# Bias rows computed four softmax units sooner in a fused attention and FFN kernel

## The chip, the cores and the metric

The kernel runs on one core of one Trainium2 chip. The metric is the device time of one execution in microseconds (us); several runs are timed and the median is given. One further execution is profiled.

## The reference, cut to what matters

Attention with a relative-position bias, then layer norm and a two-layer FFN with a residual. Batch 4, 8 heads, 576 positions, head size 64, model width 512, FFN width 2048, all float32.

```python
scores = scale * np.matmul(q, k.transpose(0, 1, 3, 2))
rel = pos[:, None] - pos[None, :]
x = (np.log1p(np.abs(rel)) / np.log1p(np.maximum(pos[:, None], 1.0)))[..., None]
bias = np.maximum(x @ w1 + b1, 0.0) @ w2          # (576, 576, 8), the same for every batch
scores = scores + bias.transpose(2, 0, 1)[None]
attn = softmax(scores)
x = (attn @ v) as (4, 576, 512)
xn = (x - mean) / np.sqrt(var + 1e-06) * g_ln
out = x + np.maximum(xn @ w_ch1, 0.0) @ w_ch2
```

The bias doesn't depend on the batch. It is computed once, kept in DRAM and read back for each batch.

## The kernel before

**Units.** The 576 query rows are cut into five chunks: 0 to 3 of 128 rows, and 4 of 64 rows. A *unit* is one batch, one chunk and one head (for chunk 4 two heads), 144 in all, numbered by `u` in the order of `ORD` (L213): chunk 4 of batches 0 and 1 (units 0 to 7), chunk 0 of all batches (8 to 39), chunk 4 of batches 3 and 2 (40 to 47), chunk 1 (48 to 79), chunk 2 (80 to 111), chunk 3 (112 to 143). The main loop (L861) writes one unit after the other; `cfirst[c]` is a chunk's first unit.

**A unit.** `qk` (L377) multiplies queries and keys on TensorE into the PSUM tile `sps`. `softmax1` (L422) subtracts the bias on VectorE into a float32 tile `t` and takes the row's minimum at once (L434), takes the exponential on ScalarE (L438) and a float16 high half (L443). `softmax2` (L446) makes the low half on VectorE (L462, L464) and transposes both by a DMA on SP's queue (L470, into `pt`, or into `wend` for every fifth unit from 35 on). `pv` (L496) multiplies with V on TensorE (L480). V's float16 halves are made by `v_max` and `split_v` (L362), eleven to four units and four units before to two units after a batch first needs them; for batch 1 that is unit 64, for batch 0 unit 72.

**The FFN.** It runs beside attention, as its tiles come ready: `ffn_w1` (L709) into `hps`, an eviction on ScalarE (L714) and a low half on VectorE (L717) into the hidden tile `hh`, then `ffn_w2` (L736) into `y`, which VectorE adds up (L747). `mbank` says how many such steps a unit gets. After unit 143 only FFN is left.

**Bias rows.** A *group* is 16 query rows of the bias for all heads, 36 in all, in the order of `gorder`: chunk 4's four (32 to 35), then 0 to 31. `bias_relu` makes four tiles `r` of the hidden layer, here one on VectorE (L162) and three on ScalarE (L160). `bias_mm`, one unit later, multiplies them with the output weights on TensorE (L181), evicts them in two parts on ScalarE into `ev` (L187), and writes `ev` to DRAM (`nb`, L211) on SP's queue. The tiles `t`, `r`, `ev` and layer norm's `u` share one pool of seven buffers. Each `r` holds 128 x (SEQ or fewer) elements, so a group's cost hangs a little on its number.

**When a group is begun.** Seven are done before the loop and five more in units 0 to 4. In later units at most one is begun, when fewer than `bneed` have been (L920 to L927). `gend[c]` is the count of groups at the end of chunk c.

**Loads.** `issue_loads` (L277) issues keys, queries and V on the queue of GpSimd, and the bias back from DRAM (`ldb`, L326) on SP's queue, seven units before the unit that needs it and only when all groups of its chunk have been through `bias_mm`. SP's queue thus carries, in order: row writes, bias loads, the transposes, and the output.

**Order.** The program's order is a starting point: a planner settles each engine's order from simulated times, and adds the waits.

Of the kernel before, what the change touches and what calls it, by code (L numbers as in the profile page):

```python
# [22 lines left out]
def kernel(  # L23
# [114 lines left out]
    def after(ins, dep):  # L138
        if dep is not None:
            tc.add_manual_dep(ins.ins, dep.ins.name,  # L140
                              mybir.DependencyInfo(mybir.DependencyClass.Sync,
                                                   mybir.DependencyReason.DATA),
                              reason="pace")
# [73 lines left out]
    for n, (b, c) in enumerate(ORD):  # L217
# [6 lines left out]
    cfirst = {c: min(u for (_, cc), u in ustart.items() if cc == c) for c in range(5)}  # L224
    gorder = [g for c in corder for g in range(8 * c, min(36, 8 * c + 8))]
    gend = {c: sum(len(range(8 * x, min(36, 8 * x + 8))) for x in corder[:corder.index(c) + 1])
            for c in range(5)}
# [178 lines left out]
    def spin(n, last=None):  # L406
        ps = ps_h.tile([128, 512], F32, tag="h", name="spin")
        ones = one_sb.bitcast(BF16)
        for _ in range(n):
            m = T.matmul(out=ps[:, 0:256], lhsT=ones[:, 0:128], rhs=ones, start=True, stop=True)  # L410
            if last is None:
                tc.keep_in_program_order(m)
            else:
                tc.add_manual_dep(m.ins, last.ins.name,
                                  mybir.DependencyInfo(mybir.DependencyClass.NoSync,
                                                       mybir.DependencyReason.DATA),
                                  reason="order")
            last = m
# [3 lines left out]
    def softmax1(u):  # L422
        if not 0 <= u < NU:
            return
        b, c, h = units[u]
        ps = st.pop(u)
        t = ep.tile([128, EW], F32, tag="e", name="t")[:, 0:SEQ]
        m = small.tile([128, 1], F32, tag="m", name="m")
        key = (seg[vis[u]], c, h)
        bias = bt[key]  # L430
        buse[key] -= 1
        if not buse[key]:
            bfree[0] += 1
        ttri[u] = V.tensor_tensor_reduce(out=halves(t), in0=ps[:, :, 0:HS], in1=halves(bias), scale=-0.125,  # L434
                               scalar=3e38, op0=ALU.add, op1=ALU.min, accum_out=m)
        if h == 0:
            l8[b, c] = small.tile([128, NH], F32, tag="l8", name="l8")
        S.activation(t, t, AF.Exp, bias=m, scale=-1.0, accum_out=l8[b, c][:, h:h + 1])  # L438
        if nat_pv(b, c):
            et[u] = (t, None)  # L440
            return
        e16 = e16p.tile([128, 1152], F16, tag="e16", name="e16")
        S.activation(e16[:, 0:SEQ], t, AF.Copy, scale=E_SCALE)  # L443
        et[u] = (t, e16)

    def softmax2(u):  # L446
        if not 0 <= u < NU:
            return
        t, e16 = et.pop(u)
        if e16 is None:  # L450
            p = ptp.tile([128, 10, 128], F16, tag="pt", name="pt")
            p = p.rearrange("p a b -> p (a b)").bitcast(F32)
            pm = ps_y.tile([128, 512], F32, tag="y0", name="ptm")
            pl = ps_h.tile([128, 512], F32, tag="h", name="ptl")
            for j in range(4):
                T.transpose(pm[:, 128 * j:128 * j + 128], t[:, 128 * j:128 * j + 128], id_sb)
            T.transpose(pl[0:64, 0:128], t[:, 512:576], id_sb)
            S.activation(p[:, 0:512], pm, AF.Copy)
            S.activation(p[0:64, 512:640], pl[0:64, 0:128], AF.Copy)
            pt[u] = p  # L460
            return
        V.scalar_tensor_tensor(out=e16[:, 640:1152], in0=t[:, 0:512], scalar=E_SCALE,  # L462
                               in1=e16[:, 0:512], op0=ALU.mult, op1=ALU.subtract)
        V.scalar_tensor_tensor(out=e16[:, 576:640], in0=t[:, 512:576], scalar=E_SCALE,  # L464
                               in1=e16[:, 512:576], op0=ALU.mult, op1=ALU.subtract)
        if u >= 35 and u % 5 == 0:
            p = wslot[NF].bitcast(F16)[:, 0:1152].rearrange("p (a b) -> p a b", b=128)
        else:
            p = ptp.tile([128, 10, 128], F16, tag="pt", name="pt")[:, 0:9]
        SY.dma_start_transpose(out=p, in_=e16)  # L470
        pt[u] = p
# [270 lines left out]
    def ffn_y():  # L742
        while yq:
            k, g, t, y, last = yq.pop(0)
            b, c = tiles[blocks[k][t]]
            x = xt[b, c].rearrange("p a d -> p (a d)")
            V.scalar_tensor_tensor(out=x, in0=y, scalar=ycs[:, g:g + 1], in1=x,  # L747
                                   op0=ALU.mult, op1=ALU.add)
            if last:
                if c < 4:  # L750
                    SY.dma_start(out=out[b, c * 128:c * 128 + 128, :], in_=x)
                else:
                    SY.dma_start(out=out[b:b + 2, 512:576, :], in_=x)
# [24 lines left out]
    def flush_lo():  # L778
        if state["lo"]:
            state["lo"]()  # L780
            state["lo"] = None
# [46 lines left out]
    def flush():  # L828
        later[0], later[1] = later[1], []
        for fn in later[0]:  # L830
            fn()
# [28 lines left out]
    u = 0  # L860
    while u < NU + 6 or jobs or cur_job or pend or yq:  # L861
        if u >= NEARLY:
            ffn_y()
        if u in FILL:
            with tc.high_priority(offset=-600):
                spin(FILL[u], lastpv[0])
        softmax1(u)
        if u == 0:
            for ins in gate:
                after(ins, ttri[0])  # L870
            gate.clear()
            gate_on[0] = False
        ustep[0] = u
        issue_loads(u)
        softmax2(u - 1)
        flush()
        for _ in range(2):
            if wload:
                load_w()
        for _ in range(8):  # L880
            if wdec and 32 - len(wdec) < 2 + (4 * max(0, u - 1) + 2) // 3:
                f, i = wdec.pop(0)
                decode_w(f, i)
                if i == 1 and f + 1 == GROUPS[GOF[f]][1]:
                    w_scale(GOF[f])
        while mm_done[0] < ngroup:
            bias_mm(gorder[mm_done[0]])
            mm_done[0] += 1
        if u % 2:
            first = qk(u + 1)  # L890
            if u >= 27 and first is not None:
                after(first, ttri[max(ttri)])
            qk(u + 2)
        while npv <= u - (LAG if u < 38 else LAG + 1):
            if pv(npv):
                lnq.append([u, len(avail_at) + len(lnq)])
            npv += 1
        for fn in todo.pop(u, []):
            fn()
        for qq in range(4):  # L900
            if wdone[0] >= 8 * qq + 8 and qq not in wready_at:
                wready_at[qq] = u
        if u < NU + 9:
            nav = len([a for a in avail_at if a <= u])
            goal = sum(2 * NF * len(bl) // 4 for bl in blocks if bl[-1] < nav)
            nxt = min((steps_av[bl[-1]] for bl in blocks if bl[-1] >= nav), default=NU + 9)
            mbank += max(0.0, (goal - (ntot - nmicro) - mbank)) / max(1, nxt - u)
            mbank = min(mbank, 2.0)
        else:
            mbank = 1.0  # L910
        flush_lo()
        ffn_y()
        while mbank >= 1.0:
            if not ffn_micro(u):
                break
            mbank -= 1.0
            nmicro -= 1
            if mbank >= 1.0:
                ffn_y()
        bneed = NP + 1 + u if u < 8 else 12  # L920
        for c in (1, 2, 3):
            bneed = max(bneed, gend[c] - 8 + min(8, (u - cfirst[c] + 34) * 8 // 24))
        if u < 28:
            bneed = min(bneed, 12)
        if ngroup < min(36, bneed):
            bias_relu(gorder[ngroup], 1 if u >= 24 else 2)
            ngroup += 1  # L927
        for _ in range(2):
            if wspl:
                split_w(*wspl.pop(0))  # L930
        for it in list(lnq):
            if it[0] == u - 1:
                ln1(it[1])
            if it[0] == u - 2:
                ln2(it[1])
                avail_at.append(u + (3 if u < NEARLY else 2))
                lnq.remove(it)
        u += 1
# [53 lines left out]
```

## Time and profile before

| | |
|---|---|
| timed runs | 686.31, 686.28, 683.54 us; median 686.28 |
| profiled execution | 679.99 us, of which the span from first to last instruction is 678.2 us |
| granted TensorE clock, mean | 0.985 of full speed |
| busy: TensorE matmul, VectorE, ScalarE | 647.7, 457.8, 392.0 us |

PE is TensorE's matmuls, PEld its weight loads, DVE VectorE, ACT ScalarE, POOL GpSimd, SP the SyncE queue that issues DMAs. A busy share tells how long an engine had an instruction running; it does not tell in which stretch it was the one that the others waited for.

### The profile page before, as it was taken

Reading aid. Unit: us, or ns where it says so; the run is one execution under the profiler, and the core shown is the slowest. Engines: PE = TensorE matmul, PEld = TensorE weight load, DVE = VectorE, ACT = ScalarE, POOL = GpSimd, SP = SyncE. Lnnn points to the kernel's source line nnn. Section 1 sums busy time; section 2 is a strip of 40 time slices with the busy share of each in tenths; the row PEclk is TensorE's granted clock in tenths of the full one; section 3 lists DMA queues with packets and bytes.
Section 4 is the critical chain, followed back from the end, with each engine's and each line's share of the span. In section 5 each row is a group of like instructions: output and inputs, shape, how many; then the busy total and the mean of one; then the engine's idle time right before and its main releaser. Section 6 shows DMA issues by size and latency. Waiting matters only on the chain.

```text
span 678.2 us, 19142 instructions
## 1 busy us (share of the span) xinstructions
PE 647.7 (96%) x7929; PEld 448.4 (66%) x7929; DVE 457.8 (68%) x1061; ACT 392.0 (58%) x777; POOL 97.4 (14%) x163
## 2 busy tenths in 40 slices
PE   6889996998999889999899999999999999999997
PEld 4447774676466666666667766666776677677775
DVE  6588999778757567686766575757576676766322
ACT  5565847478957447787764577576554455444110
POOL 5312321011000011111101110111011120000000
PEclk9989997899999999999899999999999999999999
DMA  8999885444659996868869789789996976744100
GB/s 312 294 404 331 307 294 161 143 91 115 143 122 148 223 246 156 173 156 164 172 149 239 134 183 181 136 197 181 201 200 144 166 153 125 121 98 87 33 16 17
DMA packets 186955, 117.24 MB, mean 173 GB/s; under 512 B 163956, under 2 KB 164084, under 8 KB 186868
## 3 DMA queue, kind: packets, MB, share of 16 engines
q1 hardware_dynamic: 177124, 81.00, 55.8%
q0 software_dynamic: 9600, 34.84, 16.6%
q8 instruction: 62, 1.02, 0.6%
q10 hardware_dynamic: 144, 0.18, 0.1%
q14 instruction: 25, 0.20, 0.1%
HBM read 60.51 MB, written 15.63 MB: 112 GB/s over the span
## 4 chain that ended last, share of the span: by engine, by line
PE 50%; DVE 0%; ACT 0%; issue 0%
PE hps L709 19%; PE y L736 18%; PE sps L391 6%; PE xps L480 6%; PE bps L181 1%; DVE v L369 0%; DVE x L747 0%; DVE e L462 0%; ACT e L443 0%; DVE x L516 0%; ACT t L438 0%; DVE e L464 0%
## 5 line engine op out<-in xcount | busy, mean ns | idle before, releaser
L709 PE MATMUL hps<-xT,w 128*128 128x128 f16 x3240 | 196.4, 220 | 5.8 <-DVE hh L717 2.6
L709 PEld LDWEIGHTS <-w 128*128 128x128 f16 x3240 | 184.6, 98 | 11.5 <-issue 5.2
L736 PE MATMUL y<-w,hh 128*128 128x512 f16 x810 | 189.1, 381 | 1.9 <-ACT hh L714 1.8
L438 ACT ACTIVATE t<-t,m 128x576 f32<-128x576 f32 x144 | 111.0, 771 | 132.8 <-DVE m L434 132.2
L736 PEld LDWEIGHTS <-hh 128*128 128x128 f16 x864 | 79.7, 98 | 90.6 <-ACT hh L714 3.3
L462 DVE SCALAR_TENSOR_TENSOR e<-t,e 128x512 f16<-128x512 f32 x120 | 82.8, 690 | 81.8 <-ACT e L443 81.5
L434 DVE CUSTOM_DVE_ANT_0 t<-sps,ldb 128x576 f32<-128x576 f32 x144 | 105.9, 753 | 31.4 <-PE sps L391 21.2
L391 PE MATMUL sps<-kf,qf 64*128 64x288 f32 (+1 forms) x640 | 96.6, 436 | 3.5 <-DVE m L434 3.5
L443 ACT ACTIVATE e<-t 128x576 f16<-128x576 f32 x120 | 80.8, 679 | 9.8 <-DMA pt<-e 3.5
L714 ACT ACTIVATE hh<-hps 128x512 f16<-128x512 f32 x72 | 42.0, 583 | 53.4 <-PE hps L709 47.9
L717 DVE SCALAR_TENSOR_TENSOR hh<-hps,hh 128x512 f16<-128x512 f32 x72 | 49.4, 687 | 34.0 <-ACT hh L714 33.5
L391 PEld LDWEIGHTS sps<-kf,qf 64*128 64x128 f32 (+1 forms) x640 | 48.2, 176 | 35.6 <-issue 17.5
L480 PEld LDWEIGHTS <-pt 128*128 128x128 f16 (+1 forms) x1456 | 49.3, 100 | 30.5 <-issue 24.9
L747 DVE SCALAR_TENSOR_TENSOR x<-y,ycs,x 128x512 f32<-128x512 f32 x58 | 43.4, 748 | 32.2 <-PE y L736 32.0
L480 PE MATMUL xps<-v,pt 128*128 128x64 f16 (+1 forms) x1456 | 59.0, 195 | 1.9 <-DMA pt<-e 1.1
L291 POOL DMA_DIRECT2D kf<-in_k_s_dram x56 | 31.1, 556 | 161.4 <-PE sps L391 114.3
L304 POOL DMA_DIRECT2D qf<-in_q_main_dram x32 | 18.5, 577 | 162.4 <-PE xps L480 82.6
L187 ACT ACTIVATE ev<-bps,cb_sb,par_sb 128x144 f32<-128x144 f32 (+27 forms) x48 | 26.0, 593 | 26.2 <-PE bps L181 26.0
L160 ACT ACTIVATE r<-psi_sb,par_sb 128x448 f32<-128x448 f32 (+23 forms) x72 | 39.7, 614 | 0.0
L569 POOL TENSOR_SCALAR rs<-mv 128x1 f32<-128x1 f32 x18 | 9.9, 549 | 146.3 <-DVE mv L568 138.3
L438 ACT ACTIVATION_READ_ACCUMULATOR t<-t,m 128x1 f32 x144 | 27.0, 188 | 0.0
L181 PE MATMUL bps<-r,nw_sb 128*32 128x448 f32 (+24 forms) x200 | 26.9, 494 | 0.0
(121 smaller groups left out, 641.4 us busy)
## 6 DMA issues: line engine op xcount, KB each, us to landing
kf<-in_k_s_dram POOLq DMA_DIRECT2D x56, 288.0 KB, 4.8
w<-in_w_ch_dram SPq DMA_DIRECT2D x22, 512.0 KB, 8.7
ldb<-nb SPq DMA_DIRECT2D x32, 288.0 KB, 4.5
qf<-in_q_main_dram POOLq DMA_DIRECT2D x32, 256.0 KB, 4.6
nb<-ev SPq DMA_DIRECT2D x24, 296.0 KB, 3.4
vf<-in_v_p_dram POOLq DMA_DIRECT2D x16, 320.0 KB, 7.5
out_dram<-x SPq DMA_DIRECT2D x18, 256.0 KB, 2.1
wend<-in_w_ch_dram SPq DMA_DIRECT2D x8, 512.0 KB, 4.8
```

The source lines that it names most:

```text
L160: S.activation(r[:, 0:n], psi_sb[:, 0:n], AF.Relu, bias=pr_sb[:, g4:g4 + 1], scale=1.0)
L391: m = T.matmul(out=o, lhsT=l, rhs=kk, start=True, stop=True, tile_position=(64 * hf, 64 * e))
L434: ttri[u] = V.tensor_tensor_reduce(out=halves(t), in0=ps[:, :, 0:HS], in1=halves(bias), scale=-0.125, scalar=3e38, op0=ALU.add, op1=ALU.mi ...
L438: S.activation(t, t, AF.Exp, bias=m, scale=-1.0, accum_out=l8[b, c][:, h:h + 1])
L443: S.activation(e16[:, 0:SEQ], t, AF.Copy, scale=E_SCALE)
L462: V.scalar_tensor_tensor(out=e16[:, 640:1152], in0=t[:, 0:512], scalar=E_SCALE, in1=e16[:, 0:512], op0=ALU.mult, op1=ALU.subtract)
L480: T.matmul(out=o, lhsT=p[:, m], rhs=v[:, j, a, :], start=(i == 0), stop=(i == len(ops) - 1))
L709: T.matmul(out=h[:, idx * n:idx * n + n], lhsT=w[:, wo + kk * 128:wo + kk * 128 + 128], rhs=xT[k][:, xo + kk, 0:n], start=(i == 0), stop=( ...
L714: S.activation(hh[:, 0], h, AF.Relu)
L717: V.scalar_tensor_tensor(out=hh[:, 1], in0=h, scalar=0.0, in1=hh[:, 0], op0=ALU.max, op1=ALU.subtract)
L736: T.matmul(out=yps[k][t], lhsT=hh[:, a, o:o + 128], rhs=w[:, wo:wo + 512], start=(f == f0 and i == 0), stop=(f == f1 - 1 and i == 2))
L747: V.scalar_tensor_tensor(out=x, in0=y, scalar=ycs[:, g:g + 1], in1=x, op0=ALU.mult, op1=ALU.add)
```

## The change

One constant of the formula that says how many groups should have been begun by unit u: 34 becomes 38, in the line for chunks 1 to 3.

```diff
         bneed = NP + 1 + u if u < 8 else 12
         for c in (1, 2, 3):
-            bneed = max(bneed, gend[c] - 8 + min(8, (u - cfirst[c] + 34) * 8 // 24))
+            bneed = max(bneed, gend[c] - 8 + min(8, (u - cfirst[c] + 38) * 8 // 24))
         if u < 28:
             bneed = min(bneed, 12)
         if ngroup < min(36, bneed):
```

A chunk's eight groups are spread over 24 units, one in three; the constant says how many units ahead of the chunk's first unit that begins.

## Rows read from the trace of the kernel before

**Rows 1.** The page's first part: busy us, share of span, instructions.

```profile
PE 647.7 (96%) x7929; PEld 448.4 (66%) x7929; DVE 457.8 (68%) x1061; ACT 392.0 (58%) x777; POOL 97.4 (14%) x163
```

**Rows 2.** Busy time by stretch, cut at units 28, 35, 40, 48, 56...

```profile
core 0: us, PE busy (x) PEld busy (x) DVE busy (x) ACT busy (x) POOL busy (x), PEclk, DMA share, GB/s
150.40:199.20 48.80, 46.12 (x492) 26.90 (x490) 36.11 (x78) 37.93 (x73) 4.92 (x8) 1.00 0.58 126
199.20:215.90 16.70, 16.70 (x208) 11.04 (x207) 12.43 (x32) 14.27 (x30) 0.62 (x1) 1.00 0.83 111
215.90:250.70 34.80, 31.70 (x496) 22.11 (x489) 20.48 (x49) 15.13 (x30) 5.12 (x9) 1.00 1.07 226
250.70:282.00 31.30, 30.87 (x437) 21.06 (x434) 22.49 (x54) 22.39 (x48) 4.28 (x7) 1.00 0.81 185
282.00:314.30 32.30, 32.30 (x421) 22.32 (x419) 23.92 (x58) 26.09 (x52) 4.89 (x8) 1.00 0.76 165
314.30:350.20 35.90, 33.90 (x410) 23.39 (x408) 24.83 (x59) 25.49 (x52) 5.03 (x8) 0.95 0.76 154
350.20:379.40 29.20, 29.20 (x379) 20.91 (x377) 19.67 (x46) 15.11 (x31) 2.82 (x4) 1.00 0.90 209
379.40:475.50 96.10, 96.10 (x1229) 65.18 (x1227) 62.57 (x148) 64.72 (x126) 13.27 (x24) 1.00 0.86 168
505.20:534.70 29.50, 29.50 (x386) 21.13 (x386) 19.77 (x48) 14.64 (x29) 4.93 (x8) 1.00 0.78 145
```

**Rows 3.** Timeline, group 21: start us, us, engine, line, operation, tiles.

```profile
314.41 1.54 ACT L160 ACTIVATE r<-psi_sb,par_sb 128x353 f32<-128x353 f32 x3
...
320.41 0.80 PE L181 MATMUL bps<-r,nw_sb 128*32 128x353 f32 x8
...
321.35 1.09 ACT L187 ACTIVATE ev<-bps,cb_sb,par_sb 128x352 f32<-128x352 f32 x2 [0.49 <-PE bps L181]
```

**Rows 4.** TensorE's waits from 199 to 250 us: total us, times, longest.

```profile
PE hps L709 <- DVE hh L717: 1.3, 1, 1.3
PE xps L480 <- DMA wend<-e: 0.5, 1, 0.5
```

**Rows 5.** TensorE's waits from 250.7 to 617 us, complete.

```profile
PE y L736 <- ACT hh L714: 1.6, 1, 1.6
PE xps L480 <- DVE x L543: 0.4, 1, 0.4
PE xps L480 <- DVE x L516: 0.4, 1, 0.4
```

**Rows 6.** Timeline, units 66 to 68: four rows between 322 and 334 us.

```profile
322.97 0.63 SPq L211 DMA_DIRECT2D nb<-ev  x1
...
329.41 0.76 DVE L434 CUSTOM_DVE_ANT_0 t<-sps,ldb 128x576 f32<-128x576 f32 x1 [1.29 <-DMA nb<-ev]
...
332.48 0.58 ACT L714 ACTIVATE hh<-hps 128x512 f16<-128x512 f32 x1
...
333.11 0.61 PE L736 MATMUL y<-w,hh 128*128 128x512 f16 x2 [1.57 <-ACT hh L714]
```

**Rows 7.** The tile `ev`: its row writes, issue to landing.

```profile
DMA to landing us min/median/max: 3.0/3.9/10.8
```

**Rows 8.** Busy time by stretch, 4 us each, columns as in rows 2.

```profile
330.00:334.00 4.00, 2.15 (x23) 0.69 (x20) 3.88 (x9) 3.29 (x6) 0.54 (x1) 1.00 0.48 110
334.00:338.00 4.00, 3.86 (x61) 3.85 (x61) 3.96 (x9) 2.88 (x6) 0.90 (x2) 0.57 1.14 150
```

**Rows 9.** Timeline, SP's queue and TensorE around the chunk 1 bias loads.

```profile
223.53 0.58 SPq L211 DMA_DIRECT2D nb<-ev  x1
...
228.76 1.28 SPq L326 DMA_DIRECT2D ldb<-nb  x3
...
230.21 2.01 SPq L470 DMA_TRANSPOSE wend<-e  x1
...
236.10 0.63 PE L480 MATMUL xps<-v,wend 128*64 128x64 f16 x28 [0.53 <-DMA wend<-e]
```

**Rows 10.** SP queue's waits over the span: total us, times, longest.

```profile
SPq L326 <- DMA nb<-ev: 10.5, 4, 4.6
```

## The prediction

> **What bounds the kernel now.** I read the page's busy shares first: the matrix engine has a matmul in flight for 647.7 of 678.2 us and VectorE and ScalarE stay far below it [rows 1]. A mean over the whole span hides stages, so I then cut the trace at the starts of every eighth softmax unit (the 144 instructions of L434, in order; unit 40 starts at 215.9 us, unit 48 at 250.7 us, and so on) and asked for each engine's busy time in every piece [rows 2]. The reader is to see two kinds of piece. Eight units without a bias group take 29.2 us (units 72 to 79) or 29.5 us (units 112 to 119), with no idle time on TensorE at all. Call it 29.35. Where groups fall in, the piece is longer by about 1 us for each: units 56 to 63 hold three and take 32.3, so 0.98 each; units 80 to 103 hold eight and take 96.1, so (96.1 - 3 x 29.35) / 8 = 1.0 each. The eight matmul records of one group take 0.80 us [rows 3]. So from unit 48 on a group costs its own work on TensorE and nearly nothing else, and that work is the same wherever it stands.
>
> What a shift can change is therefore only the time that TensorE loses. I listed its waits for the stretch that the change touches. From 199 to 250 us it waits 1.3 us for the low half of an FFN hidden tile and 0.5 us for a transpose [rows 4]; the piece of units 40 to 47 has 34.80 - 31.70 = 3.1 us of idle time in all [rows 2], so another 1.3 us have no releaser in the list. From 250.7 to 617 us it waits 2.4 us in all [rows 5]. Beside the idle time there is the clock: the granted share is 1.00 in every piece but that of units 64 to 71, where it is 0.95 [rows 2].
>
> That piece is the odd one. It holds three groups and should take 29.35 + 3 x 0.98 = 32.3 us, but takes 35.9, so 3.6 us are lost. The timeline shows how [rows 6]. Group 21's row write is issued at 322.97; the softmax of unit 68 on VectorE is to reuse the slot of that group's `ev` and starts at 329.41, when the write has landed, 6.4 us after its issue, against a median of 3.9 us for such writes [rows 7]. ScalarE's queue is then late, the hidden tile's eviction starts at 332.48, and TensorE stands idle until 333.11. In the 4 us after that its granted clock is 0.57 of 2.4 GHz, so part of them ran at 1.2 GHz: 0.43 x 4 = 1.72 us [rows 8]. Idle time of 2.0 us in the piece plus 1.72 makes 3.7, which is the 3.6 above.
>
> **What the change does, step by step.** I worked the formula out for every unit. With 34, the 24 groups 8 to 31 are begun in units 28 to 33, 35, 38 (chunk 1), then 49, 52, ... 70 (chunk 2), then 81, 84, ... 102 (chunk 3). With 38 the first six stay, because nothing may begin before unit 28 and one group a unit is the most; groups 14 and 15 move from 35 and 38 to 34 and 35; chunk 2 begins in 45, 48, ... 66 and chunk 3 in 77, 80, ... 98. So 18 groups move, 16 of them by four units. No instruction is added or removed: each group keeps its four relus, eight matmul records, two evictions and one row write on SP's queue, and the loads keep their units, since they are due seven units ahead of use and every chunk is now finished earlier than that.
>
> *The loads of a chunk's bias no longer wait for its last row write.* Before, group 15's write is issued at 223.53 and the loads behind it on SP only at 228.76, so SP's queue stands for about 4.6 us, and with it the transposes that feed the P.V products: the next is issued at 230.21, and TensorE waits for it at 236.10, by 0.53 us [rows 9]. Such waits add up to 10.5 us in four places [rows 10]. In the two later ones, chunks 2 and 3, nothing follows on TensorE (no row of them in [rows 5]). With three to six units between write and load the wait goes. Worth: at least 0, at most all 3.1 us of the piece's idle time; I take the one wait whose chain I can follow, -0.53.
>
> *Groups 14 and 15 stand closer.* They now follow groups 8 to 13 at one a unit. That dense stretch, units 28 to 33 within 150.4 to 199.2 us, loses 48.80 - 46.12 = 2.68 us over six groups, 0.45 each; the piece of units 35 to 39, where they are now, loses nothing, so there is nothing to win [rows 2]. Cost between 0 and 0.9; ScalarE has 14.27 of 16.7 us busy there before as after, so I take half, +0.45.
>
> *Group 16 moves into the chunk-4 piece, units 45 and 46.* Its cover there is worse for transfers and better for ScalarE: the DMA share is 1.07, the highest of the pieces, ScalarE is busy 15.13 of 34.8 us [rows 2]. Behind its write on SP's queue wait the two transposes of each unit; behind its relus and evictions on ScalarE waits the hidden tile's eviction, for which TensorE waits. Cost: 0 if it lies beside the matmuls, at most 1.54 + 1.09 = 2.63 us, three relus and two evictions in front of that eviction [rows 3]. ScalarE has room, so I take the value of a group in the dense stretch, +0.45.
>
> *The late write of units 66 to 68.* Before, groups 21 and 22 were in flight when the V split of batch 0 began (units 68 to 75); after, only group 23 can be, with its evictions in unit 67. The stall may go (-3.7) or meet group 23 instead (0). One candidate in place of two: I take half, -1.86.
>
> *Chunk 3.* Eight groups change places inside pieces where TensorE never idles: 0. A shift by four keeps their place against the loads that recur every four units. What is lost if that cover goes is a stall like the one above, 3.7 us.
>
> Sum: -0.53 + 0.45 + 0.45 - 1.86 = -1.5 us. The profiled execution took 679.99 us (span 678.2 and 1.8 around it) and would take 678.5. The median of the timed runs stands 6.3 us above that execution; the same difference on it gives 686.28 - 1.5 = **684.8 us**. About 0.5%, or 3.4 us, is what a measurement of this kernel can tell from no change, so this is no change.
>
> One rule speaks for more. TensorE's matmul share is not saturation by itself. The 0.98 us of a group against 0.80 us of matmuls leaves 0.18 us that might be a wait rather than work. The Trainium skill (Perfetto Trace Analysis, Identifying the Most-Contended Engine) says just that: matmul busy time is a poor measure of closeness to the roofline, and weight-load busy time is the better one. By it TensorE has room, since its weight loads are busy 66% of the span [rows 1]. Whether the rule bites here no row shows directly; the pieces' equal lengths speak against it.
>
> **Rivals.**
> *Faster: the stall goes and nothing comes for it.* The loss of 3.7 us goes whole and the chunk-4 piece gives back 0.53 to 3.1: 686.28 - 4.2 = 682.1, at best 679.5. For it: of 18 moved groups one alone cost TensorE such a wait. Against it: what set it off, a write beside loads and a full slot pool, stays.
> *Faster: TensorE isn't the pace.* The 0.18 us is a wait that the new places hide: 16 x 0.18 = 2.9 us on top of the sum, 681.9. Against it: 0.98 and 1.0 in pieces that lie far apart.
> *Slower: group 16's write in the crowded piece.* It lands late, the softmax that reuses the slot starts late, the hidden tile's eviction with it, and TensorE idles 2.0 us and loses 1.72 to the clock, while the old stall stays. Sum: +3.7 + 0.45 + 0.45 - 0.53 = +4.1, 690.4. It decides when that write takes over about 6 us to land, as group 21's did.
> *Slower: the planner's order.* The engines' orders are planned from simulated times, so 18 moved groups can turn other instructions round from unit 34 on; one stall of 3.7 us elsewhere gives 690.0. Nothing in the trace speaks for one.
>
> **How the numbers follow.** No change 0.50; stall gone 0.24 and not the pace 0.04, so faster 0.28; group 16's write 0.15 and the planner's order 0.07, so slower 0.22. The range runs from 680.7 (stall gone, the 0.53 and one of the 1.3 us waits gone: -5.55) to 690.4 (the third rival); some 1 in 10 is left on each side. No change alone spans 682.9 to 689.7.
>
> **What would show it.** Right: the pieces of units 72 to 111 still 29.4 us plus 1 us a group; no wait of the bias loads for `nb` writes on SP; no wait of TensorE at the transpose of unit 41. The clock below 1.00 in the piece of units 64 to 71, or in none, tells the half-counted stall's fate. Wrong: a wait of VectorE for an `ev` write in units 46 to 49 with a drop of the clock behind it, or TensorE idle in a piece of chunk 3.

## The result and the profile after

The changed kernel takes 691.28 us (median of 6 runs, 687.74 to 696.18), the kernel before 684.6 us in the same session (6 runs, 681.02 to 686.31). The ratio is 1.0123, with a 95% interval of 1.0075 to 1.0171: about 1.2% slower. The forecast was 684.8 us, no change; the time lies above its range. The profiled execution took 689.96 us, with a span of 688.2 us and a mean granted clock of 0.982, against 679.99, 678.2 and 0.985. Idle times and waits below are read from one profiled execution of each kernel, which can lie at either end of its timed runs (f1's is the slowest of 12, 692.23 us, h1's the fastest, 681.80), so a size of a few us goes by the ratios.

The page's first part hardly differs from [rows 1]:

```profile
PE 652.6 (95%) x7929; PEld 451.1 (66%) x7929; DVE 457.7 (67%) x1061; ACT 391.2 (57%) x777; POOL 95.7 (14%) x163
```

The same instructions run, and TensorE is busy 4.9 us longer, part of it at half clock. Where, the windows tell, cut at units 40, 48, 56, 64, 72, 80 and 104 as in [rows 2] (us, busy us of PE, PEld, DVE, ACT and POOL, then clock, DMA share and GB/s):

```profile
224.00:255.50 31.50, 30.20 (x445) 20.68 (x444) 20.77 (x52) 17.95 (x37) 4.18 (x8) 1.00 1.11 238
255.50:290.90 35.40, 33.90 (x497) 23.17 (x494) 22.66 (x53) 22.40 (x47) 4.68 (x9) 1.00 0.79 172
290.90:322.10 31.20, 31.20 (x406) 21.75 (x403) 24.05 (x58) 25.34 (x52) 4.65 (x8) 1.00 0.84 162
322.10:358.80 36.70, 31.77 (x402) 21.91 (x400) 23.41 (x56) 22.20 (x44) 3.56 (x8) 0.97 0.72 152
358.80:390.70 31.90, 31.90 (x387) 23.24 (x385) 20.31 (x48) 18.69 (x37) 2.75 (x4) 0.93 0.88 173
390.70:485.70 95.00, 95.00 (x1206) 64.64 (x1204) 62.20 (x146) 61.18 (x120) 13.99 (x24) 1.00 0.88 176
```

Units 80 to 103 hold seven groups now: (95.0 - 3 x 29.35) / 7 = 0.99 us each, as forecast. The bad piece is that of units 64 to 71, with 36.70 - 31.77 = 4.93 us of idle time and only one group in it, and the clock is below 1.00 in two pieces.

Pieces hold unequal work, so I also lined the two traces up by TensorE's matmul records, the n-th of one beside the n-th of the other. Up to unit 34 the changed kernel is 1.95 us late; its instructions up to there are the same, so that is scatter between executions. From there to unit 73 TensorE's order differs between the two kernels, so the differences are good to about 1 us: the changed kernel is 5.7 us late at unit 48, 6.8 at unit 64, 2.8 at unit 72 and 9.95 at unit 74 and at the end. So it loses some 3.7 us up to unit 48 and 1.1 up to unit 64, wins 4.0 over units 64 to 71, and loses 7.2 around unit 71: 8.0 in all. With the 1.95 that is the 10.0 by which the spans differ. Run f3 below, with the same order on TensorE, gives the sizes of the losses exactly.

**Place two, unit 71.** TensorE's waits from 200 us to the end of attention at 627, to be read beside [rows 4, 5], have a new head (rows 4 end at 250 us, just short of a second wait of 1.3 us for a hidden tile, in unit 47):

```profile
PE hps L709 <- DVE hh L717: 6.7, 3, 4.9
PE xps L480 <- DMA pt<-e: 1.2, 2, 1.0
PE xps L480 <- DVE x L543: 0.8, 1, 0.8
```

The hidden tile is only the last link. The timeline around 350 us shows the chain (start us, us, engine, line, operation, tiles, and in brackets the idle time before with what ended it):

```profile
340.17 0.56 SPq L753 DMA_DIRECT2D out_dram<-x  x1
340.79 0.75 SPq L211 DMA_DIRECT2D nb<-ev  x1
...
351.58 0.35 SPq L326 DMA_DIRECT2D ldb<-nb  x1
352.10 3.22 SPq L470 DMA_TRANSPOSE pt<-e  x2
...
356.12 0.68 ACT L443 ACTIVATE e<-t 128x576 f16<-128x576 f32 x1 [5.81 <-DMA pt<-e]
356.71 0.58 ACT L714 ACTIVATE hh<-hps 128x512 f16<-128x512 f32 x1
...
358.32 4.00 PE L709 MATMUL hps<-xT,w 128*128 128x128 f16 x36 [4.93 <-DVE hh L717]
```

Group 23 is chunk 2's last. Its row write goes out at 340.79, and the first bias load of chunk 2 stands right behind it on SP. It must wait until all of the chunk has landed, and leaves only at 351.58; the two transposes behind it leave at 352.10. ScalarE's high half for the next unit (L443) waits 5.81 us for them, the hidden tile's eviction stands behind it, and TensorE is idle 4.93 us. The write took 10.8 us to land, where the median of such writes is 3.7. SP's queue waits say the same of the whole span, beside the 10.5 in four places of [rows 10]:

```profile
SPq L326 <- DMA nb<-ev: 15.8, 3, 10.0
```

The idle time has an echo in the clock, as in [rows 8]:

```profile
352.00:356.00 4.00, 1.39 (x22) 0.86 (x19) 0.00 (x0) 0.00 (x0) 0.00 (x0) 1.00 0.90 184
356.00:360.00 4.00, 1.68 (x17) 1.68 (x17) 3.16 (x7) 1.54 (x3) 0.00 (x0) 0.57 1.03 190
360.00:364.00 4.00, 4.00 (x49) 3.90 (x48) 1.93 (x6) 3.03 (x7) 0.00 (x0) 0.58 0.98 237
```

TensorE was busy for 1.39 and 1.68 us of the first two windows. In the second and third its granted clock is 0.57 and 0.58 of 2.4 GHz, so part of the 1.68 + 4.00 busy us ran at 1.2 GHz. An estimate of what that cost is 0.43 x 1.68 + 0.42 x 4.00 = 2.4 us. With the 4.93 that is 7.3 us, and 7.5 is what the place costs against f3.

Why did the write take so long? The output of a chunk-4 tile went out 0.62 us ahead of it (L753, one DMA of 2 x 64 rows). From 344 to 350 us, 40 slices, the page of DMA traffic reads:

```profile
DMA  9999899210111111101119779995869867515101
GB/s 290 288 384 497 339 433 465 87 55 27 55 55 55 55 55 55 55 27 55 55 55 273 246 273 382 410 342 143 178 208 362 362 270 304 208 55 168 75 27 59
```

In the slices from 345.05 to 347.15 some one or two of 16 engines move 55 GB/s. The packets of that time are the output's, 2048 bytes each: 128 of them start between 344.39 and 349.43 us, two every 0.08 us. The row write's are of 2368 bytes: 112 of its 128 had started by 346.0, the other 16 (the share of two engines in 16) start after 349.4, when the output's last have started. So an output of 2 x 64 rows runs on two engines alone, and the row write behind it on SP's queue waits for those two with its last packets.

The Trainium skill (DMA: Bandwidth & Descriptors, Why a DMA increments its semaphore by 16 and not by 1) gives the rule: a transfer is spread over the largest number of engines, up to 16, that divides the slowest dimension of both its sides. For 2 x 64 x 512 against 128 rows that is two, and this trace agrees: the output's packets start two at a time.

**Place one, units 39 to 44.** It has two parts. In unit 39 TensorE waits 1.00 us for a transpose that stands behind the other chunk-4 output and group 15's write:

```profile
212.49 0.62 SPq L753 DMA_DIRECT2D out_dram<-x  x1
215.49 0.56 SPq L211 DMA_DIRECT2D nb<-ev  x1
216.15 2.64 SPq L470 DMA_TRANSPOSE pt<-e  x1
...
222.40 0.29 PE L480 MATMUL xps<-v,pt 128*128 128x64 f16 x4 [1.00 <-DMA pt<-e]
```

The output's 128 packets start over 6.24 us, from 213.70 to 219.94, and the transpose lands 6.2 us after its issue. In the kernel before, group 15's write goes out at 223.53 [rows 9], well behind that output, and TensorE doesn't wait in unit 39.

The other part comes from the loads. Chunk 1's bias loads no longer wait, just as forecast, but they now stand together:

```profile
223.17 2.56 SPq L326 DMA_DIRECT2D ldb<-nb  x5
225.83 0.43 SPq L751 DMA_DIRECT2D out_dram<-x  x1
226.43 6.55 SPq L470 DMA_TRANSPOSE pt<-e  x2
...
239.87 2.84 PE L709 MATMUL hps<-xT,w 128*128 128x128 f16 x48 [0.99 <-DVE hh L717]
```

Before, three loads stood together, issued at 228.76 [rows 9], and two and two came later. Now five go in a row, which takes SP 2.56 us, and the two transposes issued behind them at 226.43 and 229.41 land after 7.6 and 8.2 us. TensorE is idle 1.24 us in unit 43.

**A small place, unit 49.** Group 16's row write goes out at 253.59, and VectorE's softmax waits until a write of `ev` has landed:

```profile
258.12 0.76 DVE L434 CUSTOM_DVE_ANT_0 t<-sps,ldb 128x576 f32<-128x576 f32 x1 [1.56 <-DMA nb<-ev]
259.92 0.63 PE L480 MATMUL xps<-v,pt 128*64 128x64 f16 x28 [0.77 <-DVE x L543]
```

TensorE waits 0.77 us here (0.43 in the kernel before), and the clock stays at 1.00.

**The old stall** of units 66 to 68 [rows 6] is gone; no writer of `ev` is late there. On SP's queue the slowest write was group 21's with 6.3 us and is now group 23's with 10.8. The longest landing times of the whole tile, 10.8 us in [rows 7] and 11.5 here, belong to neither: both are of writes near 30 us on the queue of GpSimd.

```profile
DMA to landing us min/median/max: 3.0/3.7/11.5
```

### The profile page after: what moved, and what is told of

Same layout as the page of the kernel before. It is cut to its first block, busy times and chain, and to the rows that moved or that the text cites. A ratio compares the mean times of both kernels' runs of the same rounds, so it can differ in the third digit from the quotient of the medians.

```text
span 688.2 us, 19134 instructions
## 1 busy us (share of the span) xinstructions
PE 652.6 (95%) x7929; PEld 451.1 (66%) x7929; DVE 457.7 (67%) x1061; ACT 391.2 (57%) x777; POOL 95.7 (14%) x163
## 3 DMA queue, kind: packets, MB, share of 16 engines
q8 instruction: 62, 1.02, 0.6%
## 5 line engine op out<-in xcount | busy, mean ns | idle before, releaser
L434 DVE CUSTOM_DVE_ANT_0 t<-sps,ldb 128x576 f32<-128x576 f32 x144 | 105.6, 751 | 29.1 <-PE sps L391 17.4
L443 ACT ACTIVATE e<-t 128x576 f16<-128x576 f32 x120 | 80.9, 679 | 13.1 <-DMA pt<-e 10.8
L181 PE MATMUL bps<-r,nw_sb 128*32 128x448 f32 (+24 forms) x200 | 30.7, 494 | 0.0
L569 POOL TENSOR_SCALAR rs<-mv 128x1 f32<-128x1 f32 x18 | 8.5, 472 | 144.8 <-DVE mv L568 144.8
```

## The experiments

Theory A, formed from these rows, is that SP's queue makes the loss: row write, bias load and transposes stand in line, and a bias load that has to wait for a write that lands late holds up transposes that have nothing to do with it. At first I put all of it down to place two. The rival is that the groups themselves cost more where they now stand (group 16 in the chunk-4 piece, or ScalarE's queue near units 48 to 55), so that the loss is shared by the chunks and SP's queue only carries it. Ratios are to the kernel before on the same chip, with 95% intervals.

**e1: chunk 2 alone.**

```diff
-... (u - cfirst[c] + 34) * 8 // 24))
+... (u - cfirst[c] + (38 if c == 2 else 34)) * 8 // 24))
```

> Constant 38 for chunk 2 alone, 34 for chunks 1 and 3. Theory A (the loss is one place: chunk 2's last row write stands on SP's queue right behind the output of a chunk-4 tile, lands late, and the first bias load of chunk 2, right behind the write, holds the queue and so the transposes): SP's queue shows the same order here, so the wait of some 10 us for nb and TensorE's wait of some 5 us near unit 71 stay; ratio to the kernel before 1.005 to 1.013. Theory B (a spread cost of the 18 moved groups, mostly of chunks 1 and 3 and the planner's order): ratio 0.997 to 1.004, no such wait.

Measured: 690.73 us, ratio 1.0103 [1.0069, 1.0137]. The chain of place two is there again, output, row write, load, transposes:

```profile
341.18 0.56 SPq L753 DMA_DIRECT2D out_dram<-x  x1
341.80 0.97 SPq L211 DMA_DIRECT2D nb<-ev  x1
351.69 0.35 SPq L326 DMA_DIRECT2D ldb<-nb  x1
352.22 3.17 SPq L470 DMA_TRANSPOSE pt<-e  x2
```

The write takes 9.9 us, and TensorE waits 3.96 in unit 71. Chunk 2 alone makes nearly as large a loss.

**e2: chunks 1 and 3 alone** (`34 if c == 2 else 38` in the same place).

> Constant 38 for chunks 1 and 3, 34 for chunk 2. Theory A: the output and chunk 2's last write stay apart on SP's queue, no wait for nb over 5 us, ratio 0.996 to 1.005, with the stall of units 66 to 68 still there. Theory B: ratio 1.006 to 1.013.

Measured: 688.81 us, 1.0078 [1.0048, 1.0108]. No bias load waits over 2.5 us, yet 0.8% is lost: 1.80 us idle in unit 39 and 1.96 in unit 43, and the old stall of units 66 to 68 stays, since chunk 2 is as before. That one place explains everything was wrong; hence place one. The losses of e1 and e2 add up to 1.8%, more than the change's 1.2%; with these intervals that may be scatter.

**e3: the changed kernel, chunk 2's loads held back.** Each load may not go before the newest softmax instruction (L434) written so far, so the planner can't pull it forward to right behind the write.

```diff
-SY.dma_start(out=raw, in_=nbias[c][:, h, :])
+ld = SY.dma_start(out=raw, in_=nbias[c][:, h, :]); c == 2 and after(ld, ttri[max(ttri)])
```

> The changed kernel with the bias loads of chunk 2 tied to the softmax of the unit in which they are written, so that the first one is not planned right behind the last row write; every other engine's order is that of the changed kernel. Theory A: the late write stays (over 8 us) but nothing waits behind it, TensorE's wait near unit 71 goes, the clock stays at 1.00 there, some 7 to 8 us less than the changed kernel; ratio to the kernel before 0.997 to 1.005. Theory B: ratio 1.009 to 1.015, as the changed kernel.

Measured: 691.81 us, 1.0124 [1.0082, 1.0167]: a miss. The load is gone from behind the write, and the transposes are late all the same:

```profile
345.15 0.56 SPq L753 DMA_DIRECT2D out_dram<-x  x1
345.77 1.04 SPq L211 DMA_DIRECT2D nb<-ev  x1
348.27 8.66 SPq L470 DMA_TRANSPOSE pt<-e  x2
...
363.98 2.29 PE L709 MATMUL hps<-xT,w 128*128 128x128 f16 x20 [5.63 <-DVE hh L717]
```

They are issued at 348.27 and 353.32 and land after 13.4 and 9.2 us, where the median is 3.4. With no load in between, the transposes themselves stand behind the output's two engines; that the output is what delays them, f3 bears out, where it is split and the same two land after 4.1 and 5.2 us.

**e4: the changed kernel, the output split** into two DMAs of 64 rows. Their 128 packets start within 0.68 us in place of 5.04.

```diff
-SY.dma_start(out=out[b:b + 2, 512:576, :], in_=x)
+[SY.dma_start(out=out[b + n, 512:576, :], in_=x[64 * n:64 * n + 64]) for n in (0, 1)]
```

> The changed kernel with the output of a chunk-4 tile written by two DMAs of 64 rows in place of one of 2 x 64 rows; every engine's order stays. Theory A: the 2 x 64 write ran on two of the 16 DMA engines for 5 us and the row write's last packets stood behind it; split, the row write lands in 3 to 5 us, SP waits 2 to 4 us, TensorE's wait near unit 71 is gone or under 1 us; ratio 0.996 to 1.005. Rival C (the row write is late because of the key and query loads): it still takes over 8 us, ratio 1.009 to 1.015.

Measured: 689.22 us, 1.0116 [1.0081, 1.0152]: a miss. The row write lands in 4.2 us and the load holds SP for 3.1, both as expected, which rules out the key and query loads as what delayed the write. But TensorE still waits 2.9 us in unit 71 in place of 4.9, where under 1 was expected. Unit 39 no longer waits; unit 43, with the five loads in a row as before, loses 4.89 us in this execution. Neither half of place two is enough alone.

**f1: chunk 1 alone** (`38 if c == 1 else 34`).

> Constant 38 for chunk 1 alone, so that only groups 14 and 15 move. Theory A2 (two places: here the bias loads of chunk 1, which no longer wait for the last row write, are planned five in a row ahead of the transposes of units 40 and 41, which then land late; the other place is chunk 2's last row write behind the two-engine output, which is as before here): TensorE idles 2 to 5 us in units 39 to 43, transposes there take over 8 us to land, ratio 1.004 to 1.010. Rival (two groups cannot matter): ratio 0.997 to 1.003.

Measured: 685.95 us, 1.0054 [1.0022, 1.0085]. Place one by itself: five loads in a row at 225.18, transposes of 7.7 and 9.5 us behind them, TensorE idle 1.02 us in unit 39 and 2.63 in unit 43. Unit 39's wait ends at 224.59, before the loads go out, so they can't be its cause.

**f2: the changed kernel, chunk 1's loads held back** (e3's edit with `c == 1`).

> The changed kernel with chunk 1's bias loads tied to the softmax of the unit in which they are written; all other engines' orders as in the changed kernel. A2: the bunch of five is gone, transposes of units 40 to 43 land in under 8 us, TensorE idles under 1.5 us in units 39 to 44, the wait near unit 71 stays; ratio 1.004 to 1.010, 3 to 5 us under the changed kernel. Rival (the loss of units 39 to 44 has another cause): 1.010 to 1.015.

Measured: 688.42 us, 1.0068 [1.0036, 1.01]. Unit 43's idle time goes, unit 39's 1.83 stays, and so does place two with 6.08 us.

**f3: the changed kernel with both cures**, the loads of chunks 1 to 3 held back (`c and after(...)`) and the output split.

> The changed kernel with the bias loads of all of chunks 1 to 3 tied to their units and the chunk-4 outputs written by two DMAs of 64 rows. A2: neither place loses anything, the stall of units 66 to 68 of the kernel before is gone too; ratio 0.994 to 1.003. Rival (a spread cost): 1.007 or more.

Measured: 680.82 us, 0.9979 [0.9952, 1.0005]. The whole loss is gone. TensorE's waits from 200 to 627 us, complete, and SP's queue at the same output and write:

```profile
PE hps L709 <- DVE hh L717: 1.1, 1, 1.1
PE xps L480 <- DVE x L516: 0.6, 1, 0.6
```

```profile
336.79 1.58 SPq L753 DMA_DIRECT2D out_dram<-x  x2
338.47 1.34 SPq L211 DMA_DIRECT2D nb<-ev  x1
339.98 3.37 SPq L470 DMA_TRANSPOSE pt<-e  x2
...
342.47 2.84 PE L709 MATMUL hps<-xT,w 128*128 128x128 f16 x48
...
351.15 0.35 SPq L326 DMA_DIRECT2D ldb<-nb  x1
```

TensorE's order is that of the changed kernel, record for record, so the two traces line up exactly. Against f3 the changed kernel loses 1.2 us in unit 39, 1.7 in units 43 to 45, 0.8 in unit 49 and 7.5 in units 71 to 73, and wins 0.4 in unit 55 and 0.8 in chunk 3: 10.1 in all.

On SP's queue the order is still output, write, transposes, but the output's 128 packets now start within 0.62 us (340.72 to 341.34) in place of 5.04, the write lands in 4.3 us, and the load comes 12.7 us behind the write.

**f4 and f5: the kernel before** with the split alone, and with both cures (the constant at 34).

> The kernel before with the chunk-4 outputs written by two DMAs of 64 rows. A2: there the output stands apart from the row writes, so little is to be had; transposes behind it land earlier (9.6 us for the one behind the first output before); ratio 0.994 to 1.002. If the two-engine output cost the kernel before as much as the changed one, ratio under 0.992.

> The kernel before (constant 34) with the bias loads of chunks 1 to 3 tied to their units and the chunk-4 outputs written by two DMAs of 64 rows. If the moved groups are worth anything once both places are mended, this is slower than the changed kernel so mended (0.9979); if the constant is worth nothing, 0.994 to 1.000, the same as or a little under it.

Measured: f4 681.11 us, 0.9967 [0.9935, 0.9999]; f5 680.19 us, 0.9986 [0.9956, 1.0016]. So with the cures the constant is worth nothing that can be told: 0.9979 with 38, 0.9986 with 34.

**g1: chunk 2 alone with the split.**

> Constant 38 for chunk 2 alone, and the chunk-4 outputs written by two DMAs of 64 rows. If the loss of chunk 2's part is the two-engine output ahead of its last row write, the 1.0103 of chunk 2 alone comes down to 0.995 to 1.003, and that write lands in under 6 us; if chunk 2's groups cost something of their own, 1.006 or more.

Measured: 687.52 us, 1.011 [1.0071, 1.0149]: a miss. The write takes 4.5 us and the load holds SP for 4.0, and TensorE still waits 2.98 us in unit 71; the rest is in units 49 (1.80), 55 (1.46) and 97 (2.37). A short hold right ahead of transposes is a hold.

**g2: chunk 1 alone, its loads held back.**

> Constant 38 for chunk 1 alone, with chunk 1's bias loads tied to the softmax of the unit in which they are written. If the bunch of five loads is the loss of chunk 1's part, the 1.0054 of chunk 1 alone comes down to 0.999 to 1.004, TensorE's idle time of unit 43 goes and only the 1 to 2 us of unit 39, behind the two-engine output, stay; if not, 1.005 or more.

Measured: 684.02 us, 1.0039 [1.0007, 1.007], against 1.0054 for f1: the intervals overlap. Unit 43's idle time goes; 0.99 in unit 39, 1.10 in unit 45 and 1.25 in unit 47 remain (the kernel before has 0.53 and 1.30 in the last two). The transposes land late all the same, after 9.8 us behind no load and 11.7 behind one, so the five loads delay TensorE here by going first, and aren't shown to be why transposes are slow in this stretch. Over all runs with chunk 1 at 38, unit 39 waits in the six whose output is whole (the change, e2, e3, f1, f2, g2: 0.99 to 1.83 us) and not in the two where it is split (e4, f3); unit 43 waits in the five with five loads in a row (the change, e2, e3, e4, f1: 1.24 to 4.89) and not in the three where they are held (f2, f3, g2). So place one is the output's in unit 39 and the loads' in unit 43; how the 0.54% of f1 divides between them isn't settled.

**g3: chunk 3 alone** (`38 if c == 3 else 34`).

> Constant 38 for chunk 3 alone. The prediction's step: eight groups change places where TensorE never idles, ratio 0.997 to 1.003, no piece of units 72 to 111 longer than 29.4 us plus 1 us a group by more than 1 us. Rival: chunk 3 has a share of the loss, 1.004 or more.

Measured: 680.95 us, 0.9993 [0.9959, 1.0026]. Chunk 3 costs nothing.

**h1: chunk 2 alone with both cures**, the loads of chunk 2 alone held back (f3 holds those of chunks 1 to 3).

> Constant 38 for chunk 2 alone, its bias loads tied to their units and the chunk-4 outputs written by two DMAs of 64 rows. If the two together are the loss of chunk 2's part: no idle time of TensorE at unit 71, ratio 0.995 to 1.004 (the smaller waits of units 49 and 55, 1 to 2 us each, stay). If the moved groups cost something by themselves: 1.006 or more.

Measured: 685.32 us, 1.0036 [1.0008, 1.0063]. Unit 71's wait is gone and the ratio falls from e1's 1.0103, within what was expected, but not to 1. Three waits are left: 1.22 us in unit 45, one of 4.19 over units 48 and 49, and 1.16 in unit 55. The first is SP's queue again, at chunk 1: its loads, which this run doesn't hold, wait 7.5 us for group 15's write, and TensorE waits for the transpose behind them. The second is group 16's row write, issued at 250.62, with the clock down behind it (last line, columns as in [rows 8]):

```profile
255.02 0.76 DVE L434 CUSTOM_DVE_ANT_0 t<-sps,ldb 128x576 f32<-128x576 f32 x1 [2.80 <-DMA nb<-ev]
256.82 0.96 PE L480 MATMUL xps<-v,pt 128*64 128x64 f16 x28 [4.19 <-DVE x L543]
256.00:260.00 4.00, 3.18 (x34) 1.74 (x35) 2.92 (x7) 2.31 (x5) 0.00 (x0) 0.59 0.06 15
```

So the rival has a part here: some 0.4% that isn't SP's queue at unit 71. In f3, with chunks 1 and 3 moved and all three chunks' loads held, neither of the first two waits is there.

**h2 and h3: chunk 2 alone at 36 and at 40**, without cures.

> Constant 36 for chunk 2 alone: its groups two units sooner than before. On SP's queue two transposes stand between the output and the last row write. If the neighbourhood is the loss: the row write lands in under 8 us, TensorE idles under 2 us at units 70 to 72, ratio 0.997 to 1.005. If sooner costs by the unit: about half of chunk 2's 1.0103, 1.005 or more.

> Constant 40 for chunk 2 alone: its groups six units sooner than before. The last row write and the first bias load stand ahead of the output on SP's queue. If the neighbourhood is the loss: write lands in 3 to 5 us, TensorE idles under 2 us at units 66 to 72, ratio 0.997 to 1.006. If sooner costs by the unit: 1.010 to 1.016.

Measured: 679.28 us, 0.9961 [0.9935, 0.9986] at 36, and 682.42 us, 1.0001 [0.9972, 1.003] at 40. With 38 (e1) it was 1.0103. Two units less or two units more, and the loss is gone. At 40 the write takes 6.3 us, where 3 to 5 was expected, and the load holds SP for 4.5, but TensorE waits only 0.40 us in unit 69. At 36 the SP queue shows why:

```profile
330.39 0.56 SPq L753 DMA_DIRECT2D out_dram<-x  x1
335.03 3.92 SPq L470 DMA_TRANSPOSE pt<-e  x2
338.99 0.60 SPq L211 DMA_DIRECT2D nb<-ev  x1
345.80 0.35 SPq L326 DMA_DIRECT2D ldb<-nb  x1
```

Output and last write stand 8.6 us apart, with transposes in between, where it was 0.62. The write takes 6.7 us, the longest wait of a load for a write is 4.1 us, TensorE doesn't wait in unit 71, and the old stall of units 66 to 68 is gone. This run is faster than both kernels.

**i1: chunk 2 at 36 with both cures.**

> Constant 36 for chunk 2 alone, bias loads of chunks 1 to 3 held at the units of before, chunk 4's two outputs split. Chunk 2 at 36 alone gave 0.9961, and the split alone 0.9967. If each took its own loss away and the two losses are apart, the ratio is about 0.9961 x 0.9967 = 0.993. If both took away the same one, the stall of units 66 to 68, it is 0.996, and TensorE's longest wait between 250 and 617 us stays below 1.6 us. Chunk 2 at 38 with the same two edits gave 1.0036; if the groups of chunk 2 cost something by standing sooner at all, half of that shows and the ratio is near 1.0.

Measured: 678.78 us, 0.9953 [0.9921, 0.9985]. That excludes a ratio near 1.0. Between one gain taken twice (0.996) and two gains (0.993) it doesn't decide; both lie in the interval. The traces speak for one gain: against the kernel before, f4, whose order on TensorE is the same throughout, gains 2.9 us over units 68 and 69, and chunk 2 at 36 some 3.6 from unit 68 to 72, the same place, each in one execution. TensorE's waits from 200 to 617 us, complete:

```profile
PE xps L480 <- DVE x L516: 0.4, 1, 0.4
PE y L736 <- ACT hh L714: 0.2, 1, 0.2
```

There is little left to win by placing groups: 0.6 us of waits in 417.

## Why the prediction was wrong, step by step

**From unit 48 on a group costs its own work.** Right for chunk 3: 0.99 us a group after, against 0.98 and 1.0, and g3's 0.9993. It was a statement about the mean of pieces without stalls, and said nothing on where a write falls in SP's queue.

**The loads no longer wait for the last row write (-0.53).** This is the step that failed, and in both chunks. I counted the distance between write and load in units of the program, three to six, and called the wait gone. But SP's order is the planner's, and it moves the loads as soon as their data are due. In chunk 2 the first load came to stand directly behind the write, and the hold grew from 2.4 us before to 10.0. In chunk 1 the wait did go, and the freed loads went out five in a row ahead of two transposes. I listed what stands on SP's queue, but not the output's DMA as a thing that a write or a transpose could be late behind. Size, against f3: 7.5 us at place two; at place one 1.2 us in unit 39 and 1.7 in units 43 to 45, and 0.54% (3.7 us) by f1. The list of waits was also read short: the 1.3 us with "no releaser in the list" was the wait for a hidden tile in unit 47, which ended at 250.19, just behind the window of [rows 4].

**Groups 14 and 15 closer together (+0.45).** The price was taken from ScalarE, and up to unit 38 TensorE waits for nothing that it doesn't wait for before. The cost came by another way: group 15's write now stands close behind the chunk-4 output, and in unit 39 TensorE waits 1.0 to 1.8 us for the transpose behind both. With the output split it doesn't.

**Group 16 in the chunk-4 piece (+0.45).** Its work cost nothing that shows; its write did, in unit 49: VectorE waits 1.56 us for it and TensorE 0.77, 0.8 us against f3. That is the third rival's chain, and one of the signs of being wrong, but without the drop of the clock and at a fifth of its price. In h1 it came whole, 4.19 us and the clock. In the change the loss lies elsewhere: that this rival's 690.4 is near the measured time is chance.

**The late write of units 66 to 68 (half of -3.7).** The stall did go, worth some 4 us at equal work in the profiled executions: the whole price of 3.7, where I took half. It isn't fixed to the order, though: g2, with chunk 2 as before, has 0.43 us of it in its one profile. Group 23 met a stall too, later, more dearly and by another chain: SP's queue, not the slot of `ev`.

**Chunk 3 (0).** Right, by g3.

**The rivals.** "The planner's order" described what happened, one stall elsewhere, and I gave it 0.07 because nothing in the trace spoke for it. Something could have: the 128 packets of each chunk-4 output start over 7.3 and 6.7 us in the trace before too, and I looked at no output. Its price was off as well, 3.7 us for a stall that took 7.5, since I took it from a stall with 2.0 us of idle time and the one that came had 4.93. "TensorE isn't the pace" found no support.

What stays open: how f1's loss divides between the output in unit 39 and the five loads in unit 43 (g2 removes the second's idle time and not clearly its cost), and what of h1's 0.4% goes with group 16's write and what with chunk 1's loads, since no run changes one of them alone.

## What to carry to other kernels

When work that ends in a DMA is moved, write down that queue's order around each place where it lands, with every kind of DMA in it and the number of engines that each runs on: what it will stand behind, and what in-order wait will stand behind it. A load that waits at the head of a shared queue bills its wait to transfers that are ready. Where an order is planned, a shift by four is one draw among many: for chunk 2 alone 36, 38 and 40 gave 0.996, 1.010 and 1.000, so try the neighbours before calling the direction good or bad.

## What the runs showed of the hardware

The 128 packets of an output of 2 x 64 rows started over 5.04 us, two at a time, in the changed kernel's second output and over 6.24 in its first; as two DMAs of 64 rows the same bytes took 0.62 and 1.31 us in f3. The transfers behind it on SP's queue paid: a row write of 10.8 us in place of about 4, and in e3 transposes of 13.4 and 9.2 us in place of 3.4. A bias load that waited 10.0 us on SP's queue for that write kept two transposes behind it from being issued. TensorE's idle 4.93 us cost another 2.4 us, by estimate, through a granted clock of 0.57 and 0.58 in the two 4 us windows in which it came back.
